# The Sync queue's order behind attention: from a scheduler's to the program's, with two stores placed later

## The chip, the cores and the metric

The kernel runs on one core of a Trainium2 chip. The metric is the device time of one execution in microseconds (us). TensorE (PE), VectorE (DVE), ScalarE (ACT), GpSimd (POOL) and SyncE (SP) run side by side; nearly every transfer of this kernel is issued by SP, in the order in which SP's instructions stand.

## What is computed

Attention with a bias that depends on relative position, then a gated feed-forward block without a nonlinearity. The shapes are 8 batches, 8 heads, 576 positions and 64 features a head; then 4608 tokens of width 512, and an inner width of 1024.

```python
scores = scale * q @ k.T + bias          # bias: a small MLP of log1p|i-j| / log1p(i)
x = softmax(scores) @ v                  # 4608 x 512 after the heads are put together
a = x @ w1
b = x @ w2
out = ((a * b) @ w3) @ w_out
```

The kernel computes w3 @ w_out first (the *fold*) and multiplies a * b by that. The feed-forward weights arrive as 8-byte numbers and are turned into float32 on the chip. Each float32 operand is split up into a high and a low part, and a product is three matmuls (high by high, low by high, high by low).

## The kernel before

**Stages.** A bias stage writes the bias to DRAM. Attention runs over 32 units (4 head pairs by 8 batches). Its output goes to DRAM (`x_d`), and so do the softmax's reciprocal sums (`r_m`, `r_t`). Then comes the fold, and then the feed-forward block over 6 *pairs* p of 384-token columns (768 tokens a pair) and, within a pair, over 8 tiles ft of the inner width, 128 wide. Pair 0 uses plain products (`plain`, L788). Pairs 1 to 5 use a scheme with 7 products in place of 8 (`product`, L774). The second product with the folded weights is `down` (L844).

**Weights.** For weight tile t (0 to 7), `fetch_w(t, m)` fetches 512 KB of moe_w1 (m = 0) or moe_w2 (m = 1) into a tile `wi`, of which there are two, and turns it into float32: size (L195) and rest (L199) on ACT, clamp, shift and mark (L205, L209, L219) on DVE, total (L213) on POOL. A buffer of `wi` is free again when L219 has read it. `sums_w(t)` and `base_w(t)` make the split up parts (ACT L631 and L647, DVE L633, L644, L650) in a tile `wS`, of which there are three, and `sums_w` ends with the store of all 1,792 KB of it to DRAM, `w_d` (L652). Pairs 1 to 5 load these tiles back, one for each ft (`load_w`, L656, 1,792 KB each); a load waits until PE has done with the tile three before.

**Tokens.** `load_x(p, i)` fetches one of the two halves i of pair p: twice one `xr` from `x_d` (L711, 384 KB) and a row of small pieces `rb` from `r_m` and `r_t` (L423, 16 to 128 KB). Pairs 2 and 5 have 8 pieces for each `xr`, the other pairs 6. `split_x(p, i)` then multiplies the first `xr` by its `rb` and the second by its own (L734, twice in a row on DVE), takes four differences (L737) and splits up (ACT L742, DVE L744). There is one `xr` and one `rb`. The two halves of pair p + 1 are made while pair p is at ft 2 and at ft 5 (pair 1: ft 4 and ft 6 of pair 0).

**Evictions.** The sums of PE stand in two accumulators, X and Y. ACT L821 (pair 0: L806) and DVE L817 (L809) take them out, and PE may not write an accumulator before it is taken out.

**What sets the order.** The program gives each step a time from hand-written tables and emits the steps sorted by it (`put`, `until`). `drive` then runs a part of that list as a manual schedule, which fixes the order on PE, ACT, DVE and POOL as emitted. In the attention stage SP is fixed too (`drive(..., mybir.EngineType.SP)`). Behind attention `until` calls `drive(now)` without SP, and a scheduler chooses SP's order. SP's transfers take turns on eight completion semaphores, named DMAHW0 to DMAHW7 in the program's listing: a transfer waits until the one that used its semaphore before has landed.

Of the kernel before, what the change touches and what calls it, by code (L numbers as in the profile page):

```python
# [130 lines left out]
def relpos_attention_moe(  # L131
# [29 lines left out]
    def f(ap):  # L161
        return ap.bitcast(F32)
# [73 lines left out]
    def drive(plan, *more):  # L236

        E_ = mybir.EngineType
        with tc.manual_schedule(engines={E_.PE, E_.Activation, E_.DVE, E_.Pool, *more}):
            for _, _, step in sorted(plan, key=lambda e: e[:2]):  # L240
                step()

    def put(plan, steps, *times):

        def one():
            next(steps, None)
        for at in times:
            plan.append((at, len(plan), one))
# [111 lines left out]
    for i in range(2):  # L360
        t = att.enter_context(tc.tile_pool(name=f"sums{i}", bufs=1)).tile([P, 64], F32, name=f"sums{i}")
# [112 lines left out]
    later = []  # L474
# [5 lines left out]
    later = [e[:3] for e in later]  # L480

    plan = [e for e in later if e[0] < 0.0]
    later = [e for e in later if e[0] >= 0.0]
# [110 lines left out]
    later = [e for e in later if e[0] >= t_s]  # L594
# [21 lines left out]
    def fetch_w(t, m):  # L616

        if m == 0:
            big[t] = bg.tile([P, 4, 2 * P], F32, name="big")
        flat = big[t].rearrange("p s n -> p (s n)")  # L620
        src = (moe_w1, moe_w2)[m].rearrange("(c p) n -> p c n", p=P)[:, :, t * P:(t + 1) * P]
        for step in narrow(cva, src, NC * P, flat[:, m * NC * P:(m + 1) * NC * P], nc.sync, pieces=NC, signed=True):
            step()
            yield

    def base_w(t):
        x, w = big.pop(t), ups[0, t]
        w2 = bg.tile([P, 2, 2 * P], F32R, name="w2k", bufs=3)
        base[t] = (w[:, :, 0], w[:, :, 1], w2, w[:, :, 2])
        for o, y in ((w[:, :, 0:2], x[:, 0:2]), (w[:, :, 2], x[:, 3]), (w2, x[:, 2])):  # L630
            nc.scalar.activation(o[:, 0], y, AF.Copy)  # L631
            yield
            nc.vector.tensor_tensor(o[:, 1], y, f(o[:, 0]), op=ALU.subtract)  # L633
            yield

    def sums_w(t):
        x = big[t]
        w = ups[0, t] = wr.tile([P, 2, 7, 2 * P], F32R, name="wS")
        s = bg.tile([P, 4, 2 * P], F32, name="sums", bufs=1)
        for o, y, z, op in (  # L640
            (s[:, 0], x[:, 2], x[:, 3], ALU.add), (s[:, 2], x[:, 0], x[:, 2], ALU.subtract),
            (s[:, 1], s[:, 0], x[:, 0], ALU.subtract), (s[:, 3], x[:, 1], s[:, 1], ALU.subtract),
        ):
            nc.vector.tensor_tensor(o, y, z, op=op)  # L644
            yield
        for o in (0, 2):
            nc.scalar.activation(w[:, 0, 3 + o:5 + o], s[:, o:o + 2], AF.Copy)  # L647
            yield
        for o in (0, 2):
            nc.vector.tensor_tensor(w[:, 1, 3 + o:5 + o], s[:, o:o + 2], f(w[:, 0, 3 + o:5 + o]), op=ALU.subtract)  # L650
            yield
        nc.sync.dma_start(w_d[t], f(w.rearrange("p h s n -> p (h s n)")))  # L652
# [208 lines left out]
    def until(time):  # L861
        nonlocal later
        now, later = [e for e in later if e[0] <= time], [e for e in later if e[0] > time]
        drive(now)

    t_f = t_s + 11.12 + (2 * NF - 1) * PACE_F
    for i in range(2 * NF):
        hf, t = divmod(i, NF)
        t0 = t_f - (2 * NF - i) * PACE_F
# [15 lines left out]
    for t in range(NF):  # L885
        t0 = t_f + STEP0 * (t - 3) - LEAD_W * max(0, 3 - t)
        for m, (at0, d) in enumerate((((2.70, 3.35, 3.40, 3.80, 4.10, 4.90), -7.0), ((7.00, 7.65, 7.70, 8.00, 8.40, 9.40), -0.8))):
            size, rest, clamp, shift, mark, total = at0
            put(later, fetch_w(t, m), t0 + d, *(t0 + d for d in (size, rest, clamp, shift, mark, total)))
        t0 += STEP0  # L890
        put(later, base_w(t), *(t0 + d for d in (5.40, 6.00, 6.05, 6.55, 6.60, 7.00)))
        put(later, sums_w(t), *(t0 + 4.30 + 0.42 * d for d in range(4)), *(t0 + 9.70 + 0.65 * d for d in range(4)), t0 + 12.45)
    for i in range(2):
        t0 = t_s + AT_X0 + PACE_X0 * i
        put(later, split_x0(i), t0 - 5.0, *(t0 + d for d in (0.0, 1.1, 2.2, 3.3, 4.4, 5.5)))

    def start(n):
        return t_f + STEP0 * min(n, NF) + STEP * max(n - NF, 0)

    for n in range(NPR * NF):  # L900
        p, ft = divmod(n, NF)
        t0, t1 = start(n), start(n + 1)
        cs = dict(at=(p, ft))
        if p == 0:
            for j, u in AT_U.items():
                for m in range(2):
                    at(t0 + u + 2.08 * m, plain, cs, j, m)
                for k, d in AT_G.items():
                    if n == 0 and k + j == "gc":
                        d = AT_GC  # L910
# [18 lines left out]
        elif 0 < p < NPR - 1 and ft in (2, 5):  # L929
# [7 lines left out]
            )  # L937

    until(end + 1.0)
    att.close()  # L940
    wr = moe.enter_context(tc.tile_pool(name="wr", bufs=3))
    xs = moe.enter_context(tc.tile_pool(name="xs", bufs=1))
    xs1 = fx.enter_context(tc.tile_pool(name="xs1", bufs=1))
    psw.append(f1.enter_context(tc.tile_pool(name="psw1", bufs=1, space=PSUM)))
    until(t_f - NF * PACE_F + 6.0)
    f0.close()
    ps_ab = moe.enter_context(tc.tile_pool(name="ps_ab", bufs=1, space=PSUM, side="right"))
    ps_o = [moe.enter_context(tc.tile_pool(name="ps_o1", bufs=1, space=PSUM, side="right"))]
    until(t_f)
    fo.close()  # L950
    fx.close()
# [6 lines left out]
    prep.close()  # L958
    op = moe.enter_context(tc.tile_pool(name="op", bufs=NT))
    xb.append(moe.enter_context(tc.tile_pool(name="xb1", bufs=1, side="right")))  # L960
    drive(later)


_INS = ['q', 'k', 'v', 'w1', 'b1', 'w2', 'logs', 'logi', 'ilogs', 'moe_w1', 'moe_w2', 'moe_w3', 'moe_w_out']
# [53 lines left out]
```

## Time and profile before

| | us |
|---|---|
| median of 3 runs (lowest and highest) | 1070.52 (1066.74 to 1070.72) |
| the profiled execution | 1070.25 |
| its span, first to last instruction | 1068.4 |

| engine | busy us | share of the span |
|---|---|---|
| PE, matmuls | 1040.3 | 97% |
| PE, weight loads | 826.8 | 77% |
| DVE | 777.0 | 73% |
| ACT | 559.7 | 52% |
| POOL | 318.4 | 30% |

Times in the trace are counted from the start of the span. Attention ends near 450, the fold runs to 497, pair 0 from 497 to 598, and pairs 1 to 5 from there to 1063. A busy share is a mean over these stages; the waits stand in the timelines of the engines. The granted TensorE clock is 0.996 of full speed over the span.

### The profile page before, as it was taken

The numbers are of one execution on the slowest core, as the hardware profiler recorded it, in microseconds if no ns is written. First come the engines' busy times: TensorE is split into PE (matmuls) and PEld (weight loads), VectorE is DVE, ScalarE is ACT, GpSimd is POOL, SyncE is SP. The second block draws the span as 40 slices with busy tenths as digits, with TensorE's granted clock in tenths as the row PEclk, the third lists the DMA queues.
The fourth block names the chain that finished last, engine by engine and source line by source line (L and its number), as shares of the span: only waits on it lengthen the run. The fifth ranks groups of instructions, "written<-read, shape, count | busy, mean of one in ns | idle before, by whom it ended". The sixth has DMA issues, their size and how long they took to land.

```text
span 1068.4 us, 33615 instructions
## 1 busy us (share of the span) xinstructions
PE 1040.3 (97%) x13968; PEld 826.8 (77%) x13968; DVE 777.0 (73%) x1478; ACT 559.7 (52%) x1277; POOL 318.4 (30%) x342
## 2 busy tenths in 40 slices
PE   7979999999999999999999999999999999999998
PEld 2346666666666666688899999999999999999997
DVE  8989999999999999988887455444636545453333
ACT  6957877886877788855543332323323232332222
POOL 0027885882787388673220000000000000000000
PEclk9989999999999999999999999999999999999999
DMA  7987777767776766367758765565565565555431
GB/s 212 298 241 214 216 205 219 224 195 202 211 217 187 209 183 175 103 184 244 253 198 292 250 216 191 213 233 192 199 260 172 198 236 206 199 194 200 144 132 60
DMA packets 97241, 218.37 MB, mean 204 GB/s; under 512 B 22592, under 2 KB 47296, under 8 KB 90944
## 3 DMA queue, kind: packets, MB, share of 16 engines
q1 hardware_dynamic: 96656, 216.19, 62.5%
q8 instruction: 110, 1.80, 0.7%
q14 instruction: 43, 0.35, 0.1%
q10 hardware_dynamic: 432, 0.02, 0.0%
HBM read 171.45 MB, written 44.71 MB: 202 GB/s over the span
## 4 chain that ended last, share of the span: by engine, by line
PE 79%; DVE 8%; issue 6%; ACT 2%; POOL 2%; DMA 1%; SPq 0%; DVEq 0%; POOLq 0%; ACTq 0%
PE X L774 16%; PE acc L438 13%; PE Y L774 12%; PE s L342 12%; PE oc L844 9%; PE od L844 9%; DVE ts L353 4%; PE bacc L562 3%; PE Y L788 3%; PE X L788 3%; DVE pt L388 2%; POOL w3s L683 2%; ACT pp L378 1%; DMA nb<-nb_d 1%; DVE w3s L703 0%
## 5 line engine op out<-in xcount | busy, mean ns | idle before, releaser
L438 PE MATMUL acc<-pt,v 32*64 32x128 f32 (+1 forms) x9216 | 214.7, 294 | 3.7 <-issue 3.2
L378 ACT ACTIVATE pp<-ts,mx 128x576 f32<-128x576 f32 x256 | 196.0, 767 | 39.8 <-DVE mx L353 39.0
L438 PEld LDWEIGHTS acc<-pt,v 32*64 32x64 f32 x9216 | 160.8, 131 | 71.9 <-issue 54.0
L342 PE MATMUL s<-k,q 64*128 64x288 f32 (+1 forms) x1280 | 195.2, 442 | 8.1 <-DVE mx L353 6.4
L774 PE MATMUL X<-xS,wS 128*128 128x384 f32 x960 | 194.9, 338 | 0.0
L353 DVE CUSTOM_DVE_ANT_0 ts<-s,nb 128x576 f32<-128x576 f32 x256 | 182.6, 738 | 6.4 <-PE s L342 5.9
L388 DVE STREAM_TRANSPOSE pt<-pp 128x1152 f32<-128x1152 f32 x128 | 175.4, 1372 | 3.4 <-ACT pp L378 2.9
L774 PEld LDWEIGHTS X<-xS,wS 128*128 128x128 f32 x960 | 171.4, 188 | 7.0 <-ACT wos L821 0.2
L342 PEld LDWEIGHTS s<-k,q 64*128 64x128 f32 (+1 forms) x1280 | 91.0, 176 | 76.7 <-issue 35.9
L817 DVE TENSOR_TENSOR wos<-X,wos 128x384 f32<-128x384 f32 x80 | 44.6, 558 | 138.7 <-PE X L774 138.7
L774 PE MATMUL Y<-xS,wS 128*128 128x384 f32 x720 | 145.0, 336 | 0.0
L774 PEld LDWEIGHTS Y<-xS,wS 128*128 128x128 f32 x720 | 127.9, 188 | 0.1
L330 POOL COPY v<-v 64x512 f32<-64x512 f32 (+1 forms) x160 | 87.3, 564 | 127.0 <-DVE mx L353 59.6
L821 ACT COPY wos<-X 128x384 f32<-128x384 f32 x80 | 38.3, 479 | 126.2 <-PE X L774 126.2
L797 ACT ACTIVATE ghd<-wos 128x384 fp32r<-128x384 f32 x48 | 25.2, 525 | 124.6 <-DVE wos L817 105.8
L844 PE MATMUL oc<-w3s,ghc 128*128 128x512 f32 x288 | 89.8, 393 | 0.0
L844 PE MATMUL od<-w3s,ghd 128*128 128x512 f32 x288 | 89.5, 392 | 0.0
L817 DVE TENSOR_TENSOR wos<-Y,wos 128x384 f32<-128x384 f32 x80 | 44.6, 558 | 50.1 <-ACT wos L821 36.7
L225 POOL TENSOR_TENSOR wmag<-wmag 128x512 int32<-128x512 int32 x72 | 74.7, 1038 | 5.9
L797 ACT ACTIVATE ghc<-wos 128x384 fp32r<-128x384 f32 x48 | 25.2, 526 | 92.8 <-DVE wos L817 76.0
L844 PEld LDWEIGHTS oc<-w3s,ghc 128*128 128x128 f32 x288 | 53.4, 188 | 8.6
L844 PEld LDWEIGHTS od<-w3s,ghd 128*128 128x128 f32 x288 | 53.5, 188 | 8.5
(95 smaller groups left out, 1397.8 us busy)
## 6 DMA issues: line engine op xcount, KB each, us to landing
wS<-w_d SPq DMA_DIRECT2D x40, 1792.0 KB, 7.8
q<-in_q_dram SPq DMA_DIRECT2D x64, 288.0 KB, 4.2
w_d<-wS SPq DMA_DIRECT2D x8, 1792.0 KB, 6.5
v<-in_v_dram SPq DMA_DIRECT2D x96, 128.0 KB, 4.0
nb_d<-bev SPq DMA_DIRECT2D x36, 295.5 KB, 4.2
k<-in_k_dram SPq DMA_DIRECT2D x64, 144.0 KB, 3.9
x_d<-x SPq DMA_DIRECT2D x32, 288.0 KB, 3.8
xr<-x_d SPq DMA_DIRECT2D x24, 384.0 KB, 4.3
```

The source lines that it names most:

```text
L225: nc.gpsimd.tensor_tensor(d["bits"], d["bits"], d["bits"], op=ALU.add)
L330: nc.gpsimd.tensor_copy(t[64:128], t[0:64])
L342: nc.tensor.matmul(s[outs, hf, :HS], d[f"q{h}"][rows, q0:q0 + n], d[f"k{h}"][rows, :], start=True, stop=True,)
L353: nc.vector.tensor_tensor_reduce(out=halves(ts), in0=d.pop(("s", t))[:, :, :HS], in1=halves(NB[p, t]), op0=ALU.add, op1=ALU.min, scale=-1. ...
L378: nc.scalar.activation(d["p", ps][:, k * S:(k + 1) * S], ts, AF.Exp, bias=mx, scale=-1.0, accum_out=SUMS[u // 4 % 2][:, col:col + 1],)
L388: nc.vector.transpose(o, st[u].pop(("p", ts)))
L438: nc.tensor.matmul(acc[outs, a, c0:c0 + 32 * (t1 - t0)], d["v", b][rows, h], pt_[rows, t0:t1, 32 * b:32 * b + 32], start=(b == 0), stop=(b ...
L774: nc.tensor.matmul(acc, w[:, l, W_AT[n], i * P:(i + 1) * P], x[:, r, X_AT[n]], start=(k in "125" and i == 0 and m == 0), stop=(i == 1 and ...
L788: nc.tensor.matmul(acc, w[:, l, i * P:(i + 1) * P], x[:, r, 2 * k + "cd".index(j)], start=(n == 0), stop=(n == 11),)
L797: nc.scalar.activation(st[n], st["g" + j], AF.Copy)
L817: nc.vector.tensor_tensor(st[o], x, y, op=op)
L844: nc.tensor.matmul(d["o", j, t], l[:, sl], folded[ft][r], start=(ft == 0 and n == 0), stop=(ft == NF - 1 and n == 2),)
```

## The change

SP is put under the program's order in the two calls of `drive` behind attention, and the store of weight tile 1 is given a time 12.0 later and that of weight tile 2 a time 4.0 later. No instruction is added or removed.

```diff
     def until(time):
         nonlocal later
         now, later = [e for e in later if e[0] <= time], [e for e in later if e[0] > time]
-        drive(now)
+        drive(now, mybir.EngineType.SP)
@@
-        put(later, sums_w(t), *(t0 + 4.30 + 0.42 * d for d in range(4)), *(t0 + 9.70 + 0.65 * d for d in range(4)), t0 + 12.45)
+        put(later, sums_w(t), *(t0 + 4.30 + 0.42 * d for d in range(4)), *(t0 + 9.70 + 0.65 * d for d in range(4)),
+            t0 + 12.45 + (0.0, 12.0, 4.0)[t] if t < 3 else t0 + 12.45)
@@
-    drive(later)
+    drive(later, mybir.EngineType.SP)
```

The order of the instructions on PE, DVE, ACT and POOL is the same in both programs; SP issues the same 743 transfers in another order. Two places show how.

**SP around the stores of weight tiles 0 to 2.** `wi_..<-in_moe_w1` is the first fetch of a weight tile, `in_moe_w2` the second; the first row is the second fetch of tile 1. Before:

```order
L187 DMA wi_9397<-in_moe_w2_dram 128x4x256 [waits DMAHW5_49,DVE_49]
L187 DMA wi_9509<-in_moe_w1_dram 128x4x256 [waits DMAHW6_49,DVE_49]
L711 DMA xr_10154<-x_d0_88 128x768 [waits DMAHW7_49]
L652 DMA w_d0_8994<-wS_9417 128x3584 [waits DMAHW0_49,DVE_49]
L187 DMA wi_9565<-in_moe_w2_dram 128x4x256 [waits DMAHW5_49,DMAHW1_49,DVE_49]
L423 DMA rb_10155<-r_m0_92 64x320 [waits DMAHW2_49]
L423 DMA rb_10155<-r_t0_96 64x2x32 [waits DMAHW3_49]
L423 DMA rb_10155<-r_m0_92 64x384 [waits DMAHW4_49]
L423 DMA rb_10155<-r_m0_92 64x320
L187 DMA wi_9657<-in_moe_w1_dram 128x4x256 [waits DMAHW6_49,DVE_49]
L652 DMA w_d1_8995<-wS_9590 128x3584 [waits DMAHW7_49,DVE_49]
L187 DMA wi_9684<-in_moe_w2_dram 128x4x256 [waits DMAHW1_49,DMAHW0_49,DVE_49]
```

After:

```order
L187 DMA wi_9397<-in_moe_w2_dram 128x4x256 [waits DMAHW5_49,DVE_49]
L652 DMA w_d0_8994<-wS_9417 128x3584 [waits DMAHW6_49,DVE_49]
L187 DMA wi_9509<-in_moe_w1_dram 128x4x256 [waits DMAHW7_49]
L187 DMA wi_9565<-in_moe_w2_dram 128x4x256 [waits DMAHW5_49,DMAHW0_49,DVE_49]
L187 DMA wi_9656<-in_moe_w1_dram 128x4x256 [waits DMAHW7_49,DMAHW1_49,DVE_49]
L652 DMA w_d1_8995<-wS_9590 128x3584 [waits DMAHW2_49,DVE_49]
L187 DMA wi_9683<-in_moe_w2_dram 128x4x256 [waits DMAHW3_49,DMAHW0_49,DVE_49]
L187 DMA wi_9768<-in_moe_w1_dram 128x4x256 [waits DMAHW4_49,DMAHW1_49,DVE_49]
L187 DMA wi_9822<-in_moe_w2_dram 128x4x256 [waits DMAHW3_49,DVE_49]
L652 DMA w_d2_8996<-wS_9710 128x3584 [waits DMAHW6_49]
```

The store of tile 0 (`w_d0`) now stands ahead of the first fetch of tile 2; the store of tile 1 still stands between the two fetches of tile 3; the store of tile 2 has gone behind the second fetch of tile 4; pair 1's `xr` and `rb` have gone behind the first fetch of tile 7.

**SP in pair 1, around the load of the weight tile for ft 3** (`wS_10792<-w_d3`), with the token loads of pair 2 (`xr_10821`, `rb_10822`). Before:

```order
L711 DMA xr_10821<-x_d2_90 128x768 [waits DMAHW5_49]
L423 DMA rb_10822<-r_m2_94 64x128 [waits DMAHW6_49]
L423 DMA rb_10822<-r_t2_98 64x2x32 [waits DMAHW7_49]
L423 DMA rb_10822<-r_m2_94 64x512 [waits DMAHW0_49]
L423 DMA rb_10822<-r_t2_98 64x2x32 [waits DMAHW1_49]
L856 DMA out_0_dram<-osb_10768 128x512 [waits DMAHW2_49,Activation_49]
L856 DMA out_0_dram<-osb_10777 128x512 [waits DMAHW3_49,DVE_49]
L856 DMA out_0_dram<-osb_10789 128x512 [waits DMAHW4_49,Activation_49]
L656 DMA wS_10792<-w_d3_8997 128x3584 [waits DMAHW5_49,PE_49]
L423 DMA rb_10822<-r_m2_94 64x128 [waits DMAHW6_49]
L423 DMA rb_10822<-r_t2_98 64x2x32 [waits DMAHW7_49]
L423 DMA rb_10822<-r_m2_94 64x512 [waits DMAHW0_49]
```

After:

```order
L856 DMA out_0_dram<-osb_10789 128x512 [waits DMAHW6_49,Activation_49]
L656 DMA wS_10792<-w_d3_8997 128x3584 [waits DMAHW7_49,PE_49]
L711 DMA xr_10821<-x_d0_88 128x768 [waits DMAHW0_49]
L423 DMA rb_10822<-r_m0_92 64x128 [waits DMAHW1_49]
L423 DMA rb_10822<-r_t0_96 64x2x32 [waits DMAHW2_49]
L423 DMA rb_10822<-r_m0_92 64x512 [waits DMAHW3_49]
L423 DMA rb_10822<-r_t0_96 64x2x32 [waits DMAHW4_49]
L423 DMA rb_10822<-r_m0_92 64x128 [waits DMAHW5_49]
L423 DMA rb_10822<-r_t0_96 64x2x32 [waits DMAHW6_49]
L423 DMA rb_10822<-r_m0_92 64x512 [waits DMAHW7_49]
L423 DMA rb_10822<-r_t0_96 64x2x32 [waits DMAHW0_49]
L711 DMA xr_10821<-x_d2_90 128x768 [waits DMAHW1_49]
```

All 18 transfers of the half now follow the load of that weight tile in one block; before, most of them stood ahead of it. The other half of each pair moves in the same way, behind the load for ft 6.

## Rows read from the trace of the kernel before

**Rows 1.** Windows view: stretch, length, busy us (and instructions) of each engine, clock, DMA.

```profile
497.50:512.20 14.70, 11.43 (x62) 10.26 (x60) 13.12 (x26) 7.52 (x16) 3.09 (x4) 1.00 0.92 299
512.20:1059.00 546.80, 546.80 (x2850) 510.38 (x2851) 283.40 (x516) 172.29 (x359) 11.80 (x9) 1.00 0.57 202
```

**Rows 2.** Timeline of PE, start of pair 0: start, duration, instruction [idle before <- what ended it].

```profile
509.23 2.38 PE L788 MATMUL X<-xB,wS 128*128 128x384 f32 x12 [2.64 <-ACT wos L806]
...
512.18 1.31 PE L788 MATMUL Y<-xB,w2k 128*128 128x384 f32 x6 [0.58 <-DVE wos L809]
```

**Rows 3.** Timeline of ACT, from the end of the fold into pair 0.

```profile
488.76 0.65 ACT L195 ACTIVATE wmag<-wi 128x512 f32<-128x512 f32 x1
...
507.59 0.67 ACT L195 ACTIVATE wmag<-wi 128x512 f32<-128x512 f32 x1 [1.83 <-DMA wi<-in_moe_w_dram]
...
508.71 0.46 ACT L806 COPY wos<-X 128x384 f32<-128x384 f32 x1
...
555.67 0.67 ACT L195 ACTIVATE wmag<-wi 128x512 f32<-128x512 f32 x1
```

**Rows 4.** Timeline of SP: issue of the fetches (L187) and stores (L652).

```profile
475.06 3.55 SPq L187 DMA_DIRECT2D wi<-in_moe_w_dram  x2
...
484.70 0.34 SPq L652 DMA_DIRECT2D w_d<-wS  x1
...
498.16 0.34 SPq L652 DMA_DIRECT2D w_d<-wS  x1
499.56 0.37 SPq L187 DMA_DIRECT2D wi<-in_moe_w_dram  x1
...
540.26 6.22 SPq L187 DMA_DIRECT2D wi<-in_moe_w_dram  x2
```

**Rows 5.** Tile view of rb: issues at 611.0 alone, and their time to landing.

```profile
L423 SPq DMA_DIRECT2D rb<-r_m x1: 457/457/457, 611.0 to 611.0; - x1
...
DMA to landing us min/median/max: 8.3/8.3/8.3
```

**Rows 6.** Timeline of DVE, end of the fold.

```profile
494.35 0.42 DVE L205 TENSOR_SCALAR wmag<-wmag 128x512 f32<-128x512 f32 x1
...
495.75 2.38 DVE L650 TENSOR_TENSOR wS<-sums,wS 128x512 fp32r<-128x512 f32 x2
```

**Rows 7.** DMA view: issues, KB each, median us from issue to landing.

```profile
wS<-w_d SPq DMA_DIRECT2D x40, 1792.0 KB, 7.8
...
wi<-in_moe_w_dram SPq DMA_DIRECT2D x16, 512.0 KB, 3.9
...
rb<-r_t SPq DMA_DIRECT2D x64, 16.0 KB, 2.8
```

**Rows 8.** Tile view of rb, whole span: durations of an issue in ns, min/median/max.

```profile
L423 SPq DMA_DIRECT2D rb<-r_t x64: 599/600/1382, 457.8 to 913.7; - x64
```

**Rows 9.** Waits view of SP, 497 to 512: total us, times, longest.

```profile
SPq L423 <- DMA wi<-in_moe_w_dram: 1.7, 1, 1.7
```

**Rows 10.** Timeline of SP in pair 1: loads of weight tiles for ft 3 and ft 6.

```profile
610.58 0.40 SPq L656 DMA_DIRECT2D wS<-w_d  x1
...
644.46 0.38 SPq L656 DMA_DIRECT2D wS<-w_d  x1
```

**Rows 11.** Timeline of DVE in pair 1, ft 2 and ft 5.

```profile
624.42 1.82 DVE L734 TENSOR_TENSOR xr<-xr,rb 128x768 f32<-128x768 f32 x2
...
628.68 0.56 DVE L817 TENSOR_TENSOR wos<-X,wos 128x384 f32<-128x384 f32 x1 [0.44 <-PE X L774]
629.65 0.56 DVE L817 TENSOR_TENSOR wos<-Y,wos 128x384 f32<-128x384 f32 x1 [0.41 <-PE Y L774]
...
632.80 0.56 DVE L817 TENSOR_TENSOR wos<-X,wos 128x384 f32<-128x384 f32 x1 [0.79 <-PE X L774]
...
658.90 1.81 DVE L734 TENSOR_TENSOR xr<-xr,rb 128x768 f32<-128x768 f32 x2
```

**Rows 12.** Timeline of PE in pair 1, at the start of ft 3.

```profile
633.64 1.20 PE L774 MATMUL X<-xS,wS 128*128 128x384 f32 x6
```

## The prediction

> **What bounds the kernel now.** I read the busy shares first, then the windows behind attention, then the timelines of PE, ACT and SP where PE has a gap, and last the timelines of pairs 1 to 5, where the change moves most transfers. The reader should see two things. From 512.2 to 1059.0 PE is busy for 546.80 of 546.80 us, while the DMA engines are at 0.57 [rows 1]: PE is the bound there, no transfer shows, and a better order of transfers has nothing to win. From 497.5 to 512.2 PE is idle for 14.70 - 11.43 = 3.3 us [rows 1], in two gaps of 2.64 and 0.58 [rows 2]. The first is ended by ACT's L806 at 508.71, which takes out X; ACT comes to it late since L195, just ahead, waited until 507.59 for a fetched weight tile [rows 3]. That is the second fetch of tile 3, issued at 499.56 behind the store of tile 1 at 498.16 [rows 4]: eight us to land, against a median of 3.9 for its size [rows 7]. The second gap is the tail of the same delay, on DVE. So 3.2 us are what a better order behind attention can win, 0.3% of the time. The attention stage has SP in the program's order already, and the last stores stand in the same order in both kernels.
>
> **The change part by part.** No instruction is added, and the order on PE, DVE, ACT and POOL stays. I go through SP's places in order of time; sums are made on the profiled execution, 1070.25, which lies 0.27 below the median of the runs shown, 1070.52.
>
> *The store of tile 1.* Its number in the table is raised by 12.0, but in the built order it still stands between the two fetches of tile 3, and it waits for the same DVE step. Issue, landing and the gap of 2.64 stay: 0. Were the fetch to land in 3.9 us it would be there at 503.5, long before ACT needs it, and both gaps would go: -3.2. I take 0, since the order shows the cause unmoved.
>
> *The store of tile 0 ahead of the first fetch of tile 2.* The store waits for DVE until 484.70; the fetch, now second of the two at 475.06 and out by 478.6 [rows 4], follows at 485.05. A transfer issued 0.45 us behind a 1,792 KB one (610.58, [rows 10]) took 8.3 us to land [rows 5], so this one lands near 493.4. ACT's L195, at 488.76 now [rows 3], waits till then. Behind it stand L199 and the two L647, which then end near 495.7. DVE needs L195's result at 494.35, and the two L647 one after the other from 495.75 on [rows 6]. The cover is just enough: 0.2 us, between 0 (the store lands in time) and 1.0 (the fetch lands another us later). This delay adds to the gap of 2.64, since the second fetch of tile 3 waits for a buffer that DVE then frees later.
>
> *The store of tile 2 behind the second fetch of tile 4, and fetches 5 to 7.* The fetches come free of it, but PE has no gap there: 0, from 0 to 0. The second fetch of tile 7 now stands behind pair 1's 14 token transfers. Issued in turn from 540.7 at 0.64 us each (0.60 busy [rows 8] and the space between), they put it at 549.7 instead of some 546, and with 3.9 us [rows 7] it lands at 553.6, two us before ACT's L195 at 555.67 wants it [rows 3, 4]: 0.
>
> *Token loads in pairs 1 to 4.* This is the large move. Take pair 1, first half. The weight tile load of ft 3 goes out at 610.58 as now, since it waits for PE [rows 10]. All 18 token transfers follow. Eight semaphores go round, so the seventh `rb` waits until the weight tile has landed, and the eighth until the first `xr` has. That such a wait holds SP is seen once in the trace: an `rb` waited 1.7 us for the fetch eight transfers ahead [rows 9]. The `xr`, issued at 611.03, lands 8.3 us later if its size adds nothing (619.3), or 1.1 us more by its share of the weight tile's 7.8 (620.4). From there the eighth `rb`, the second `xr` and 8 `rb` have to be issued: 9 intervals of 0.64, 5.8 us, and the last, a 16 KB one, takes 2.8 to land [rows 7]. So the second multiplication can start between 627.9 and 629.0; now it starts at 624.42 + 0.91 = 625.33 [rows 11]. DVE is held up by 2.6 to 3.7 us. Behind it on DVE stand four L737 and the evictions, and before the eviction at 632.80 DVE has 0.44 + 0.41 + 0.79 = 1.64 us of idle time that ends on PE [rows 11]. PE's block at 633.64 may not write X before that eviction is done, 0.28 us earlier now [rows 12]. So PE loses 2.6 - 1.92 = 0.7 to 3.7 - 1.92 = 1.8; I take 1.3, the middle. The load for ft 4, which queues behind, is issued some 5 us later than now and is not needed for two ft more: 0.
>
> In the second half the weight tile goes out at 644.46 [rows 10], and the multiplications start at 658.90 [rows 11]: 14.44 us later, in place of 13.84. DVE is held up by 0.6 us less: 0.1 to 1.2 us for PE. No output stores run ahead of this tile, so it should land sooner: I take 0.3.
>
> Pairs 2 and 5 have 8 pieces to an `xr`, and are loaded in pairs 1 and 4: two places of each kind. Pairs 3 and 4 have 6: three intervals or 1.9 us less, which puts the loss at 0 (0 to 0). Pair 1's halves are of that kind, too: 0.
>
> A page speaks against this price. The Trainium skill, in DMA: Bandwidth & Descriptors, Anatomy of one DMA, fits a transfer as 2.0 us plus bytes over 436e3 (for the GpSimd path), which by my arithmetic is 6.2 us for a weight tile, where this trace has 7.8 [rows 7]. By it the loads would come 1.6 us earlier, no place would cost more than 0.2, and the sum would be some +0.4.
>
> **Sum.** 0.2 + 2 x 1.3 + 2 x 0.3 = +3.4 us, from 0 + 1.4 + 0.2 = +1.6 to 1.0 + 3.6 + 2.4 = +7.0. On the profiled execution: 1073.7, from 1071.9 to 1077.3; against the median of the runs it is 1073.9. I say 1073.5.
>
> **The rivals.** *Slower, with nothing absorbed.* If DVE's idle time does not take up the hold (a late eviction delays ACT's copy, that delays DVE's next step, and PE's other accumulator waits too), each place costs the whole wait: twice 3.2 and 2.2, and in pairs 2 and 3, where 1.9 us less are held, twice 1.3 and 0.3. That is 14 us: 1084. It decides once a hold outlasts the 1.92 us by so much that the next ft starts late as well. Against it: the two accumulators are taken out by two engines, and DVE is busy for only 283 of 547 us [rows 1].
>
> *Faster: the gap goes after all.* Right behind the fetch that ACT waits for, SP now issues pair 1's `rb` and `xr`; after the change they are gone from there. If transfers share the engines and do not queue, the fetch lands sooner and most of the 3.2 us are won: with no loss later, 1067. For it: the DMA share is 0.92 there [rows 1]. Against it: a small `rb` behind a weight tile took 8.3 us [rows 5], as a queue served in turn would have it, so what comes behind the fetch cannot have held it up.
>
> *The change shows nothing.* The order moves, but each transfer still lands before it is wanted, as would be if the weight tile ahead landed 2 us sooner than I read: 0 to +1, so 1070.5 to 1071.5.
>
> **How the numbers follow.** 0.5%, some 5.4 us, is about what a measurement of this kernel can tell from no change. Chances: forecast 0.66 (a tenth of it beyond +5.4), nothing shows 0.15, faster by up to 3.2 us 0.09, slower with nothing absorbed 0.10. The gain cannot pass 0.5% by any mechanism here, which leaves 0.03 for a stray time. So faster 0.03, slower 0.10 + 0.07 = 0.17, within 0.5% 0.80. The range leaves out most of the slow rival and the last part of the gain: 1067.5 to 1077.5.
>
> **What would show it.** Right: in the timeline of DVE the second L734 of pairs 1 and 4 has an idle time of 2 to 4 us before it, ended by a transfer of `rb` or `xr`; PE's blocks some 9 us later have gaps near 1 us, two large and two small or none; SP waits for landed transfers inside the block of token loads. L195 at 488.76 waits some 4 us, and the gap of 2.64 is still there, a little larger. Wrong: no gap on PE behind 512 (nothing shows, or the weight tiles land sooner); gaps at all eight places, or of 3 us each; or the gap at 506.5 is gone.

## The result, and the profile after

The changed kernel was compared with the kernel before twice. The first comparison gave 1076.89 us against 1068.77: ratio 1.0067, 95% interval 1.0047 to 1.0086. A later one, beside experiments, gave 1073.94 against 1069.64: ratio 1.0040, interval 1.0025 to 1.0056. The change costs 0.4 to 0.7%. The forecast was 1073.5, or +0.28%, and both times lie inside its range of 1067.5 to 1077.5; "within 0.5%" had the chance of 0.80, and the two comparisons lie on either side of that bound. Ratios and intervals are those recorded for each comparison; the quotient of the two medians differs from the ratio by up to 0.16% (here 1.0076 and 1.0040).

The profiled execution of the changed kernel took 1077.75 us, 7.5 more than that of before. From its page: the span, the busy times, and the chain of work that ended last, by engine; under it the same chain before.

```profile
span 1075.9 us, 33615 instructions
...
PE 1044.4 (97%) x13968; PEld 828.7 (77%) x13968; DVE 776.6 (72%) x1478; ACT 559.5 (52%) x1277; POOL 318.8 (30%) x342
...
PE 70%; DVE 12%; issue 6%; DMA 6%; ACT 3%; SPq 2%; POOL 1%; DVEq 0%; ACTq 0%; POOLq 0%
```

```profile
PE 79%; DVE 8%; issue 6%; ACT 2%; POOL 2%; DMA 1%; SPq 0%; DVEq 0%; POOLq 0%; ACTq 0%
```

Transfers, which did not show behind 512 before [rows 1], now hold 6% of the chain, where they had 1%. The timeline of DVE in pairs 1 and 4 shows where: the second of the two multiplications L734 waits for a piece of `rb`; before, both ran as one pair [rows 11].

```profile
624.76 0.95 DVE L734 TENSOR_TENSOR xr<-xr,rb 128x768 f32<-128x768 f32 x1
630.54 0.96 DVE L734 TENSOR_TENSOR xr<-xr,rb 128x768 f32<-128x768 f32 x1 [4.83 <-DMA rb<-r_t]
...
666.35 0.96 DVE L734 TENSOR_TENSOR xr<-xr,rb 128x768 f32<-128x768 f32 x1 [2.37 <-DMA rb<-r_t]
...
910.18 0.96 DVE L734 TENSOR_TENSOR xr<-xr,rb 128x768 f32<-128x768 f32 x1 [3.65 <-DMA rb<-r_t]
...
946.33 0.96 DVE L734 TENSOR_TENSOR xr<-xr,rb 128x768 f32<-128x768 f32 x1 [3.44 <-DMA rb<-r_t]
```

SP's timeline at the first of these places. The weight tile goes out at 610.91, where it was 610.58 [rows 10]; the seventh `rb` waits until it has landed, 10.35 us later; the last `rb` goes out at 627.81, and L734 starts 2.7 us behind it.

```profile
610.91 0.41 SPq L656 DMA_DIRECT2D wS<-w_d  x1
611.37 0.68 SPq L711 DMA_DIRECT2D xr<-x_d  x1
...
615.91 0.60 SPq L423 DMA_DIRECT2D rb<-r_t  x1
621.26 0.45 SPq L423 DMA_DIRECT2D rb<-r_m  x1
...
627.81 0.60 SPq L423 DMA_DIRECT2D rb<-r_t  x1
```

PE behind these holds: a gap ended by the late eviction L817. In pair 1 it is followed by two blocks of 1.94 and 2.07 us in place of 1.20 [rows 12].

```profile
634.02 1.31 PE L774 MATMUL X<-xS,wS 128*128 128x384 f32 x6 [1.98 <-DVE wos L817]
635.17 1.94 PE L774 MATMUL Y<-xS,wS 128*128 128x384 f32 x6
636.91 2.07 PE L774 MATMUL X<-xS,wS 128*128 128x384 f32 x6
...
913.67 1.33 PE L774 MATMUL X<-xS,wS 128*128 128x384 f32 x6 [0.78 <-DVE wos L817]
916.40 1.32 PE L774 MATMUL X<-xS,wS 128*128 128x384 f32 x6 [0.35 <-DVE wos L817]
```

Windows of the same execution (columns as in [rows 1]): the granted clock, 1.00 up to the end of the gap, is 0.50 in 636 to 638, that is 1.2 in place of 2.4 GHz.

```profile
632.00:634.00 2.00, 0.04 (x1) 0.00 (x0) 1.97 (x5) 0.00 (x0) 0.00 (x0) 1.00 1.00 416
634.00:636.00 2.00, 1.98 (x10) 1.99 (x11) 1.32 (x3) 0.52 (x1) 0.00 (x0) 0.84 0.42 179
636.00:638.00 2.00, 2.00 (x8) 1.85 (x7) 1.25 (x3) 0.52 (x1) 0.00 (x0) 0.50 0.80 229
```

At pair 0's start PE has these gaps, 3.81 us in all against 3.22 [rows 2]:

```profile
500.51 2.39 PE L788 MATMUL X<-xB,wS 128*128 128x384 f32 x12 [0.60 <-ACT wos L806]
...
506.77 2.38 PE L788 MATMUL X<-xB,wS 128*128 128x384 f32 x12 [1.43 <-ACT wos L806]
...
510.93 1.31 PE L788 MATMUL Y<-xB,w2k 128*128 128x384 f32 x6 [1.78 <-DVE wos L809]
```

The 0.60 more is a lead that PE gives back: its block of 497.51 starts 1.98 us earlier than before, DVE's steps 1.25.

I laid the starts of PE's blocks side by side, after minus before. The block of 512.18 starts 1.25 us earlier in this execution. The blocks up to 516.79 then lose 1.59 us, in a stretch at a clock of 0.50 again.

```profile
513.00:515.00 2.00, 2.00 (x7) 1.71 (x7) 1.98 (x4) 0.00 (x0) 0.96 (x1) 0.50 1.13 455
```

The four places lose 3.80, 0.28, 1.65 and 1.45 us, and nothing else behind 520 loses 0.2. That is -1.25 + 1.59 + 7.18 = +7.5, all of the 7.5. The -1.25 is chance: at 432 us, in attention, where all orders agree, the traces of the twelve other runs lie between 4.9 us earlier and 1.8 us later than before, as much as the change costs. So a loss is read from PE's blocks behind that place, and not from the span of one execution.

### The profile page after: what moved, and what is told of

The parts are those of the page before. It is cut to its first block, busy times and chain, and to the rows that moved or that the text cites. A ratio compares the mean times of both kernels' runs of the same rounds, so it can differ in the third digit from the quotient of the medians.

```text
span 1075.9 us, 33615 instructions
## 1 busy us (share of the span) xinstructions
PE 1044.4 (97%) x13968; PEld 828.7 (77%) x13968; DVE 776.6 (72%) x1478; ACT 559.5 (52%) x1277; POOL 318.8 (30%) x342
## 4 chain that ended last, share of the span: by engine, by line
PE 70%; DVE 12%; issue 6%; DMA 6%; ACT 3%; SPq 2%; POOL 1%; DVEq 0%; ACTq 0%; POOLq 0%
PE X L774 13%; PE acc L438 12%; PE s L342 11%; PE Y L774 10%; PE od L844 8%; PE oc L844 8%; DVE ts L353 4%; PE bacc L562 3%; DVE pt L388 3%; PE Y L788 3%; DMA xr<-x_d 3%; PE X L788 3%; SPq L423 2%; DMA rb<-r_t 1%; ACT pp L378 1%
## 5 line engine op out<-in xcount | busy, mean ns | idle before, releaser
L817 DVE TENSOR_TENSOR wos<-X,wos 128x384 f32<-128x384 f32 x80 | 44.6, 557 | 132.5 <-PE X L774 132.3
L817 DVE TENSOR_TENSOR wos<-Y,wos 128x384 f32<-128x384 f32 x80 | 44.6, 558 | 48.7 <-ACT wos L821 37.1
```

Source lines behind the costliest of these rows:

```text
L817: nc.vector.tensor_tensor(st[o], x, y, op=op)
```

## Experiments

Each ratio is against the kernel before, run beside it on the same chip.

| run | ratio | 95% interval |
|---|---|---|
| e1_late_pairs_only | 1.0030 | 1.0011 to 1.0049 |
| e2_start_only | 0.9987 | 0.9969 to 1.0005 |
| e3_loads_ahead | 0.9975 | 0.9951 to 0.9999 |
| e5_all_moved | 0.9997 | 0.9976 to 1.0017 |
| r5_after_again (the changed kernel) | 1.0040 | 1.0025 to 1.0056 |
| r6_evict_first | 0.9972 | 0.9955 to 0.9989 |
| r7_evict_first_store_old | 0.9957 | 0.9942 to 0.9973 |
| r8_second_halves | 1.0017 | 0.9996 to 1.0037 |
| r9_evict_only | 0.9975 | 0.9955 to 0.9994 |

**The last part of SP's order alone, and all but it.** e1 is the kernel before with SP ordered in the last `drive` only; e2 is the changed kernel with that call given back to the scheduler. The last part holds the token loads of pairs 2 to 5, the weight tile loads and the output stores.

```diff
 # e1, on the kernel before
-    drive(later)
+    drive(later, mybir.EngineType.SP)
 # e2, on the changed kernel
-    drive(later, mybir.EngineType.SP)
+    drive(later)
```

> The kernel before, with Sync in the program's order only in the last part (token loads of pairs 2 to 5, weight tile loads, output stores); the start of pair 0 is as before. Theory A (the token loads behind the weight tile hold up VectorE, and the granted clock falls behind some of the gaps on TensorE): waits of 2 to 5 us before the second multiplication in pairs 1 and 4, none over 1 us in pairs 2 and 3, 4 to 7 us lost on TensorE there, time 1073 to 1076. Theory B (the order of stores and fetches at the start of pair 0 is what costs): 1068 to 1070, no gaps behind 512.

> The changed kernel with the last part given back to the scheduler: only the stores and fetches around pair 0 and pair 1's token loads are in the program's order. Theory A: no gap on TensorE in pairs 1 to 4; what is left is the start of pair 0, 0 to 2.3 us: 1068 to 1071. Theory B: all of the loss, 1074 to 1077.

e1 costs 0.30%, e2 nothing that can be told. In e1 the second L734 is held by 2.55, 2.46, 3.49 and 3.60 us in pairs 1 and 4, and PE loses 4.1 there; a hold of 1.15 in pair 3, over the 1 us that was expected, costs it nothing. In e2 nothing is held in pairs 1 to 4. So the loss is in the last part; which transfers make it, the next run shows.

**The loads ahead of the weight tile again, SP ordered everywhere.** The program's time of the token loads is set 4 us earlier, so that they stand ahead of the load for ft 3 and ft 6.

```diff
-                later, split_x(p + 1, i), t0 - 8.0, ...
+                later, split_x(p + 1, i), t0 - 12.0, ...
```

> The changed kernel with one number altered: token loads of pairs 2 to 5 4.0 us earlier in the plan, which puts them ahead of the weight tile for ft 3 and ft 6 in place of behind it. All of Sync stays in the program's order. Theory A: the waits before the second multiplication go, and TensorE's gaps in pairs 1 to 4 with them; the weight tile behind the block is issued some 11 us later and still lands 3 to 4 us before it is needed: 1068 to 1071. If it lands late instead, gaps appear at the start of ft 3 and ft 6, 2 us or more each, and the time is 1075 or more. Theory B: 1074 to 1077, as the changed kernel.

No hold and no gap is left in pairs 1 to 4, and the kernel is no slower than before. Its ratio of 0.9975 has an interval that ends at 0.9999, its medians differ by 0.1%, and behind 520 its PE blocks keep their distance to those of before within 0.02 us; a gain is not shown. It is the place of the token loads behind the weight tile that costs, not the fixed order.

**The gap at pair 0's start: is it the store?** e5 is e3 with two stores at other places on SP: that of tile 0 behind the first fetch of tile 2 again, that of tile 1 behind the second fetch of tile 3, which ACT waits for.

```diff
-            t0 + 12.45 + (0.0, 12.0, 4.0)[t] if t < 3 else t0 + 12.45)
+            t0 + 12.45 + (1.5, 7.65, 4.0)[t] if t < 3 else t0 + 12.45)
```

> As the run with the loads ahead, and two numbers of the table of stores altered (1.5, 7.65, 4.0 in place of 0.0, 12.0, 4.0), so that in the built order the store of tile 0 stands behind the first fetch of tile 2 again, and the store of tile 1 really stands behind both fetches of tile 3. Theory A, with the store as cause of the gap at the start of pair 0: the 2.6 us gap shrinks to under 1 us: 1065 to 1068. If that gap has another cause: as the run with the loads ahead, 1068 to 1071.

The fetch came in time (ACT's L195 at 506.36 waits for nothing), and nothing was won. ACT, PE and the granted clock of e5:

```profile
506.36 0.66 ACT L195 ACTIVATE wmag<-wi 128x512 f32<-128x512 f32 x1
...
508.00 2.38 PE L788 MATMUL X<-xB,wS 128*128 128x384 f32 x12 [0.72 <-ACT wos L806]
512.88 2.29 PE L788 MATMUL Y<-xB,w2k 128*128 128x384 f32 x6 [2.50 <-DVE wos L809]
...
512.00:514.00 2.00, 1.12 (x3) 1.12 (x4) 1.41 (x4) 1.14 (x3) 1.27 (x1) 0.64 0.36 75
514.00:516.00 2.00, 2.00 (x8) 2.00 (x8) 1.58 (x4) 0.92 (x2) 0.00 (x0) 0.50 1.05 349
```

The gap went from X to Y. The reason is DVE's own queue. Its timeline has L644, which starts when POOL lets it, and, with no idle time between, the L809 that takes out Y. In order: before, after, e5.

```profile
500.93 0.76 DVE L644 TENSOR_TENSOR sums<-big 128x256 f32<-128x256 f32 x2 [1.40 <-POOL big L213]
...
511.58 0.55 DVE L809 TENSOR_TENSOR wos<-Y,wos 128x384 f32<-128x384 f32 x1
```

```profile
499.68 0.76 DVE L644 TENSOR_TENSOR sums<-big 128x256 f32<-128x256 f32 x2 [1.41 <-POOL big L213]
...
510.33 0.55 DVE L809 TENSOR_TENSOR wos<-Y,wos 128x384 f32<-128x384 f32 x1
```

```profile
501.63 0.76 DVE L644 TENSOR_TENSOR sums<-big 128x256 f32<-128x256 f32 x2 [1.40 <-POOL big L213]
...
512.29 0.54 DVE L809 TENSOR_TENSOR wos<-Y,wos 128x384 f32<-128x384 f32 x1
```

From the one to the other it is 10.65, 10.65 and 10.66 us, wherever the fetch lands, and PE's Y block starts 0.6 us behind L809 in all three. What PE waits for X ahead of that, it does not wait for Y. Other runs bear it out: from L644 to L809 it is 10.64 to 10.66 us in e1, e2, e3, r5, r8 and r11, too, and the two gaps are 1.99 and 1.19 us in e1, 1.69 and 1.53 in e2, 1.65 and 1.57 in r8, each time 3.2 in all as before.

**The changed kernel again, and its second halves alone.** r8 is the changed kernel with the first halves' loads ahead.

```diff
-                later, split_x(p + 1, i), t0 - 8.0, ...
+                later, split_x(p + 1, i), t0 - (8.0 if i else 12.0), ...
```

> The changed kernel itself, once more, beside the kernel before. Theory (the loss sits in the token loads of pairs 1 to 4, and its size follows how soon the weight tile ahead of them lands): ratio 1.003 to 1.007; DVE is held 2.5 to 5 us before the second L734 in both halves of pair 1 and 3 to 4 us in both of pair 4; PE loses 4 to 7 us at these four places and under 0.5 us elsewhere behind 520. Rival (the surplus over the kernel in which only the last drive is ordered, 1.0067 against 1.003, comes from the order of the start): pairs 1 to 4 lose 4 us as there, and PE loses 2 to 3 us more than before between 497 and 520.

> The changed kernel with the token loads of the first halves put ahead of the weight tile again, those of the second halves left behind it. Theory (each half is held by itself, a second half like a first): DVE is held 2.4 to 3.6 us before the second L734 at ft 5 of pairs 1 and 4 and not at ft 2; PE loses 0.2 to 0.7 us in pair 1 and 1.0 to 1.7 us in pair 4; ratio 1.000 to 1.002. By the prediction's term: held 2 to 3.1 us, 0.3 us lost at each, ratio 0.998 to 1.000. Rival (the holds of a second half are the first half's delay handed on): no hold at ft 5 either.

In r5 PE loses 5.7 us at the four places, and from 501.77 to 520 its blocks keep their distance to before, but for a shift between the two gaps; the rival falls. The hold in the second half of pair 1, 2.15 us, is shorter than expected. In r8 only the second halves are held, by what was expected. What each hold costs, over the kernels (us held, and us that PE lost, by the starts of its blocks against before; r10 and r11 follow below):

| place | after | r5 | e1 | r8 | r10 | r11 |
|---|---|---|---|---|---|---|
| pair 1, first half | 4.83, 3.80 | 4.96, 3.11 | 2.55, 0.63 | none | 3.82, 1.88 | 3.18, 1.25 |
| pair 1, second half | 2.37, 0.28 | 2.15, 0.05 | 2.46, 0.39 | 2.53, 0.47 | 3.22, 1.13 | 2.98, 0.89 |
| pair 3, first half | 0.26, 0.00 | 1.05, 0.00 | 1.15, 0.00 | none | 0.82, 0.00 | 2.50, 0.56 |
| pair 4, first half | 3.65, 1.65 | 3.33, 1.33 | 3.49, 1.50 | none | 3.42, 1.43 | 3.63, 1.65 |
| pair 4, second half | 3.44, 1.45 | 3.21, 1.23 | 3.60, 1.61 | 3.04, 1.05 | 3.11, 1.13 | 2.62, 0.63 |

Of the 23 losses 22 are the hold less 1.85 to 2.1 us, and the holds under 1.2 cost nothing. The exception is the first: 2.8 by that rule, and 1.0 more with the clock at half, at which two blocks were longer by 0.74 and 0.87 (and a second gap of 0.36, which r5 has there, is missing). r5 has a gap of 2.19 and keeps its clock:

```profile
627.00:629.00 2.00, 0.00 (x0) 0.00 (x0) 1.97 (x5) 0.00 (x0) 0.00 (x0) 1.00 0.96 401
629.00:631.00 2.00, 1.85 (x10) 1.85 (x11) 1.31 (x4) 0.52 (x1) 0.00 (x0) 1.00 0.47 201
```

**The evictions of pair 0's first tile put ahead.** r6 is e5, r7 is e3 (the store of tile 1 as in the changed kernel), r9 is the kernel before, each with three times changed: ACT's L806 goes ahead of L195 and L199, and DVE's L809 ahead of L800, two L650, L205, L219 and L209.

```diff
-                    at(t0 + u + 2.08 * m, plain, cs, j, m)
+                    at(t0 + u + (0.6 if n == 0 and j == "d" else 2.08) * m, plain, cs, j, m)
@@
+                    if n == 0 and k + j in ("pd", "gd"):
+                        d = 0.62 if k == "p" else 0.64
+                    if n == 0 and k + j == "lc":
+                        d = 6.90
```

> The kernel with all stores moved and the loads ahead, and now the second pair of sums of pair 0, tile 0, is taken out earlier: ACT L806 ahead of L195 and L199, DVE L809 ahead of L800, two L650, L205, L219 and L209. Theory (the gap at pair 0's start is the queue on DVE and ACT, not the store): the gaps of 0.72 before X and 2.50 before Y go, 3.0 us or more, and with them the stretch at half the granted clock, another 1 us or so; the ratio falls from 0.9997 to 0.995 to 0.997. Rival (the stretch is bound by the weight tile's preparation, whoever is first): the gap moves to the down product or to the next tile's matmuls, and the ratio stays at 0.9975 or above.

> The same early eviction on the kernel with the loads ahead, with the store of tile 1 where the changed kernel has it, between the two fetches of tile 3. Theory (the store delays only what stands behind L195 on ACT, and the eviction no longer does): no gap of over 0.7 us at pair 0's start, the same time as the run above within 0.15%. Rival (the store still counts, through the late fetch): the fetch that lands at 507 to 508 delays L199, total and the next tile, a gap of 1 to 2 us shows before the matmuls of the next tile, 0.1 to 0.2% above the run above.

> The kernel before with the early eviction alone, SP's order left as it was. Theory (the 3.2 us at pair 0's start are the queue on DVE and ACT, and SP's order has nothing to do with them): both gaps of before, 2.64 and 0.58, go but for some 0.6; ratio 0.996 to 0.998, as with the loads ahead (0.9957). Rival (the scheduler's late fetch of tile 3, landing near 507.6, now holds L195, L199, total and the next tile): a gap of 1 to 2 us before the next tile's matmuls, near 512 to 520, ratio 0.998 to 1.000.

Both gaps went in all three; 0.57 is left in r6 and r7, before the block ahead. In r7 L809 stands at 503.78, 7.01 us behind L644, and X and Y follow without a gap:

```profile
502.26 2.28 PE L788 MATMUL X<-xB,wS 128*128 128x384 f32 x12
504.38 1.31 PE L788 MATMUL Y<-xB,w2k 128*128 128x384 f32 x6
```

r7 beats both kernels: 1065.4 us, 4.2 below the kernel before. r9, with the scheduler's order, gets a new gap two tiles on, as its rival had it in form, since ACT's L195 waited until 517.96 for a fetch. It is not the fetch that the rival named but the second of tile 4, which went out at 509.47 behind the store of tile 2 at 508.56; the change puts that store behind it.

```profile
517.96 0.66 ACT L195 ACTIVATE wmag<-wi 128x512 f32<-128x512 f32 x1 [2.89 <-DMA wi<-in_moe_w_dram]
...
519.60 2.39 PE L788 MATMUL X<-xB,wS 128*128 128x384 f32 x12 [1.79 <-ACT wos L806]
```

r7's profile has no such gap, so SP's order does have a worth there once DVE's queue is out of the way; the intervals of r6, r7 and r9 overlap, and do not settle how much.

**Two kernels with one execution each.** r10 is the changed kernel with the table at (0.0, 0.0, 0.0), so that the stores of tiles 1 and 2 each stand ahead of one more fetch; r11 is e1 again. They took 1079.91 and 1074.58 us, which as single times settle nothing; their traces are read.

> The changed kernel with the two stores at their old times (the table 0, 0, 0): SP is under the program's order, nothing else. Theory (the stores' places move PE by little): gaps at pair 0's start of 3.2 to 4.5 us in all, holds in pairs 1 to 4 as in the changed kernel. On the long landing at the first half of pair 1 (10.35 and 10.34 us to the seventh rb in two looks, 7.3 with only the last drive ordered): if it belongs to what stands on SP in that place, it is 10.3 here too; if it hangs on the execution's history, it is 7.2 to 8.7.

> The kernel with only the last drive ordered, once more, for the wait ahead of the seventh rb in the first half of pair 1: 7.3 us in the first look. If the length is a property of the program, 7.2 to 7.5 again, and a hold of 2.4 to 2.7 before the second L734; if it comes and goes with the execution, anything from 7.2 to 10.4.

r10 shows what the table is for: without it PE's gap at pair 0 is 5.18 us, more than was expected, with the clock at 0.50 behind it. ACT's L195 waited 4.59 us for a fetch behind the store of tile 1, and DVE stood idle for 2.38 of it behind ACT's L701; from L644 to L809 it took 13.14 us. An order of the transfers can lengthen DVE's stretch, then, though none that was tried makes it shorter.

```profile
511.71 4.21 PE L788 MATMUL X<-xB,wS 128*128 128x384 f32 x12 [5.18 <-ACT wos L806]
...
511.00:513.00 2.00, 1.29 (x4) 1.29 (x5) 2.00 (x4) 0.66 (x2) 0.17 (x1) 0.50 0.80 254
```

The seventh `rb` of pair 1's first half went out 9.46 us behind the weight tile in r10, and 7.76 in r11, against 10.35 and 10.34 in the changed kernel and 7.30 in e1. r10 meets neither of its two expectations; r11 lies outside the 7.2 to 7.5 that were expected of a property of the program, and inside the 7.2 to 10.4 of something that comes and goes. The wait was longer in all three traces in which all of SP is ordered than in the two with the last part alone, though SP issues the same transfers in the same order there; that it belongs to the program is not shown, and the cause stays open.

## Why the prediction was right or wrong

**The mechanism held.** The loss sits where the prediction put it: the token loads behind the weight tile, the hold before the second L734, DVE's slack of 1.92 us (the table says 1.85 to 2.1), then PE's gap. e1, which has this part alone, has the ratio 1.0030, 3.2 us, and loses 4.1 in its profile; the term was 2 x 1.3 + 2 x 0.3 = 3.2. That agreement is partly luck, since two of its sizes were off. That the whole change lies inside the range is luck in part, too: at 0.4 to 0.7% it cost 1.4 to 2.4 times the forecast.

**The step that failed: the sizes of the holds.** *First halves*, 2.6 to 3.7 us: the five holds of pair 4, 3.33 to 3.65, fit; those of pair 1 are 2.55 to 4.96, and in the changed kernel 4.83 and 4.96. The working took the first `xr` to land 8.3 to 9.4 us after its issue; there it took 10.8, behind a weight tile that took 10.35. The upper bound was also too low by its own words: the share of 384 in 1,792 KB of 7.8 us is 1.7 and not 1.1, which makes the longest hold 4.2. *Second halves*, 2.0 to 3.1 us, with a loss of 0.3 taken: pair 1 was held 2.15 to 3.22 and lost 0.05 to 1.13, pair 4 2.62 to 3.60 and lost 0.63 to 1.61. "It should land sooner" came true: the seventh `rb` went out some 7.5 us behind the tile, against 10.35 and 8.64 in the first halves. But DVE got its last `rb` later: L734 starts at 946.33, 4.6 us behind the last issue in pair 4, and 3.1 behind that in pair 1 (666.35), where the sum had 2.8, the median of such a piece. Why that piece is slower there stays open. The two issues on SP:

```profile
663.21 0.60 SPq L423 DMA_DIRECT2D rb<-r_t  x1
...
941.76 0.60 SPq L423 DMA_DIRECT2D rb<-r_t  x1
```

**What the sum lacked: the clock.** No term had it. In the profiled execution it cost 1.59 us at pair 0's start and 1.0 in pair 1; r5 has neither, and its PE loses 5.7 us against 7.2 + 1.6. The two comparisons of the changed kernel differ in that direction, 1.0067 and 1.0040, but their intervals overlap, and one profile each does not prove it the cause. Nor does the fall at pair 0's start belong to the change: r11, with the order of before there, has it, too.

**The reading of pair 0's start was wrong.** "3.2 us are what a better order behind attention can win" took the second gap for the tail of the first. It is the end of DVE's queue: [rows 1] had DVE at 13.12 of 14.70 us, and that was the sign. e5 removed the late fetch and won nothing; r6 and r7 moved the eviction and won the gaps. So the cost of 0 for *the store of tile 1* came out, though for another reason (the stretch ends with DVE in either order), and the -3.2 beside it, for a fetch in time, was not to be had: e5 had its fetch in time. "The gap of 2.64 still there, a little larger" is wrong in form: it became 1.43, and the one behind it 1.78.

***The store of tile 0*** (0.2): ACT's L195 waited 4.12 us, as foretold, and the cover held whole.

```profile
491.71 0.67 ACT L195 ACTIVATE wmag<-wi 128x512 f32<-128x512 f32 x1 [4.12 <-DMA wi<-in_moe_w_dram]
```

DVE's L650 behind it starts at 494.48, 1.27 us earlier than in [rows 6], and L644 at 499.68, 1.25 earlier: DVE lost nothing, as all its steps there lie 1.25 us earlier in this execution. *Pairs 2 and 3*, put at 0 from 0 to 0: no loss of 0.2 us in either profile of the changed kernel, but r11 was held 2.50 us in pair 3 and lost 0.56, so that term had a range. Of pair 1's own halves the second was held 1.58 us (583.13) and cost nothing, as foretold. *Fetches 5 to 7*: none.

**The rivals.** *Nothing absorbed* falls by the table. *Faster: the gap goes*: it did not, though not for the reason given, since no order that was tried won it while DVE's queue stood there. The premise that was argued away ("what comes behind the fetch cannot have held it up") has the runs for it: from the issue of the second fetch of tile 3 to ACT's L195 it is 7.4 to 8.1 us in the four traces with pair 1's `rb` and `xr` right behind it (before, e1, r9, r11), and 6.8 to 7.1 in the six without them and with the store still ahead (after, r5, e2, e3, r7, r8). *Shows nothing* falls with e1. The lower price of a weight tile that was weighed, an estimate of 6.2 us by the Trainium skill (DMA: Bandwidth & Descriptors, Anatomy of one DMA, whose fit is for the GpSimd path and not for SP), is met by no weight tile of pairs 1 to 5 whose landing the trace of the changed kernel records. From the tile view of wS:

```profile
DMA to landing us min/median/max: 7.2/7.6/8.4
```

## What to carry to other kernels

Before a stall is given a worth, look at the other engines in the same stretch: if one is busy nearly throughout, as DVE was here, the gap may only move to what that engine ends, and its order is what has to change. A step held up costs its engine's hold less the slack behind it, and that slack can be read from the idle times before the next evictions; the hold itself needs the whole chain of issues and landings, each with its spread, not with its median. Ordering a queue by the program is only as good as the times in the program: the same order cost 0.4 to 0.7% with the small loads behind a large one, and nothing that can be told with them 4 us earlier.

## What was not expected of the hardware

A gap of about 2 us on PE can bring the granted clock to 0.50 for some 3 us: behind 1.98 and 1.78 us in the changed kernel, behind 2.50 in e5, where the next two blocks took 2.29 and 1.69 us in place of 1.31 and 1.22. It need not: 2.64 in the kernel before and 2.19 in r5 left it at 1.00. The size of the gap alone does not decide it: r11 has a gap of 2.68 where the kernel before has 2.64, with the same order on all engines up to there, and its clock fell to 0.50 for part of the stretch shown.

```profile
507.92 3.17 PE L788 MATMUL X<-xB,wS 128*128 128x384 f32 x12 [2.68 <-ACT wos L806]
...
509.00:511.00 2.00, 2.00 (x9) 1.74 (x8) 1.78 (x5) 0.19 (x1) 0.61 (x1) 0.55 1.04 328
```

It cost 0.8 us in r11 and 1.0 to 1.6 at the three places of the changed kernel and e5, as much as a gap of this change.
